# Attention states in 64-column tiles and cross products in 64x64 tiles, with two head pairs swapped and four reorderings, in a fused retention and SwiGLU-like block

## The chip, the core and the metric

The kernel runs on one core of a Trainium2 chip. The core has a matrix engine (TensorE, PE in the profile, with its weight loads shown as PEld), three elementwise engines (VectorE, DVE; ScalarE, ACT; GpSimd, POOL) and SyncE (SP), which here issues nearly all DMAs. The metric is the device time of one execution in microseconds. Before the change it is 308.35 us, the median of three runs (308.25 to 308.38).

## The reference

`q`, `k`, `v` have 8 batches, 8 heads, 576 positions and 64 columns. The reference is a retention layer followed by a two-matrix block:

```python
scores = q @ k.T / sqrt(64)
ret    = scores * gamma[h] ** (s - t)   for s >= t, else 0      # gamma[h] = 1 - 2 ** (-5 - h)
x      = ret @ v                        # laid out as (8 * 576) rows of 8 heads * 64 columns
h      = x @ w_in                       # 512 -> 2048
out    = (h * sigmoid(beta * h)) @ w_out  # 2048 -> 512
```

Since the decay is a power, `gamma ** (s - t)` splits into a factor of the query row and one of the value row. So the first 512 positions of a batch can be done in four chunks of 128 with a running state: the output of a chunk is its own masked product plus `q` times the sum of `k.T @ v` over the chunks before it.

## The kernel before

**Tiles.** A batch has four chunks (`CB = 4`); the last 64 positions of the eight batches are gathered in pairs into four "tail" blocks of 128 rows, entries `(None, c)` of the list `seq`. The two-matrix block works on 512 rows at a time: `up` (line L430) makes 16 tiles of the hidden layer, four matmuls of 512 columns each, and ScalarE evacuates each with a Silu (L432); `down` (L463) makes 4 row tiles of the output, 16 matmuls of 512 columns each. Heads are kept in four pairs `p`, each pair filling 128 partitions; `j` is the head within a pair.

**One batch of attention.** For chunk `i`: `pre` casts `k` to `kn` and scales `v` to `vn` (POOL, L279 and L261), `pre_q` scales `q` (L253), and a DMA transpose (`x_q`, `x_k`, L287) or PE (`t_q`, `t_k`) turns them. `a_sc` (L329) makes scores with 64 rows of contraction per head, DVE masks them into `R` (L334). `a_st` (L413) adds `kn.T @ vn` to the state in PSUM: one matmul of 128x128 per head pair, of which only the two 64x64 blocks on the diagonal are wanted. ACT copies these two blocks (L418, one copy for each `j`) into `sbds` or, after the last chunk, `ends`; those tiles are zero off the diagonal. `a_O` (L385) makes the chunk's own product, 64 output columns per head. `a_cross` (L371) adds `q` times the state, one 128x128 block-diagonal matmul per pair. `a_x` (L401) copies the sum to `xT`, which `up` reads. The tails use `ends` of two batches (L368).

**Order.** The order on every engine is written out by hand. `fill` is a list of `up` and `down` steps; `merged` walks it and, before step number n, runs all attention steps whose due number is n or less. `u1` is the number at which the `up` steps of batch 1 begin, `d0` that of the `down` steps of batch 0, `base[n]` that of the n-th block. While block n is computed, the attention of batch n+1 is woven in: `first` (state and scores of two chunks) and `outputs` (the products of all four chunks). Batches 0 and 1 have their own hand-written order.

**Loads.** SP issues DMAs in program order. At the start it loads `q`, `k`, `v` of batch 0, then `w_in` in seven pieces (L176), then `w_out` in four (L194), each into a ring of four buffers, then batch 1 and so on. A piece of `w_in` is cast by DVE and POOL (L190) as four slices `ko` of 128 rows; `ko` is also the head pair that the slice multiplies.

Of the kernel before, what the change touches and what calls it, by code (L numbers as in the profile page):

```python
# [11 lines left out]
F32 = mybir.dt.float32  # L12
BF16 = mybir.dt.bfloat16
# [6 lines left out]
def kernel(  # L20
# [10 lines left out]
    nc = tc.nc  # L31
    B, H, S, D = q.shape
# [3 lines left out]
    P = 128  # L36
    HP = H // 2
    KO = d_model // P
# [12 lines left out]
    seq = []  # L51
# [19 lines left out]
    QB = 2  # L71
    q_tiles, kv_tiles = {}, {}

    def load_q(b):

        if b >= B:
            return
        t = stage.tile([P, H, CB, D], F32, name="qn", tag="qn", bufs=2)
        for u in range(2):
# [3 lines left out]
        q_tiles[b] = t  # L83

    def load_kv(n, js=(0, 1)):

# [61 lines left out]
    causal2 = consts.tile([P, P], BF16, name="causal2")  # L148

    NS = 3  # L150
    sbds = [consts.tile([P, HP, P], BF16, name=f"sbd{i}") for i in range(NS)]
    ends = [consts.tile([P, HP, P], BF16, name=f"end{i}") for i in range(4)]
    for s in sbds + ends:
        nc.vector.memset(s[:], 0.0)


    w_in_sb = wpool.tile([P, KO, d_ff], BF16, name="w_in_sb")
# [125 lines left out]
    def heads(t, p):  # L283
        return t[:, 2 * p:2 * p + 2, :].rearrange("p h d -> p (h d)")
# [63 lines left out]
    def O_of(i, p):  # L348
        Os = live[i]["O"]
        return Os[p // 2][:, p % 2] if split(i) else Os[0][:, p]  # L350

    def opens(i, p):
        return p == 0 or split(i) and p == 2

    def a_cross(i, first):

        b, c = seq[i]
        if first:
            new_O(i)
        if c == 0 and b is not None:  # L360
            return
        for p in range(HP):
            rhs, view = q_cols(i, slice(0, P), p)
            O = O_of(i, p)
            if b is None:
                for x in range(2):
                    r = slice(x * TL, (x + 1) * TL)
                    nc.tensor.matmul(O[:, r], ends[(2 * c + x) % 4][:, p, :], rhs[:, r],  # L368
                                     start=False, stop=True, skip_group_check=True)
            else:  # L370
                nc.tensor.matmul(view(O), sbds[(c - 1) % NS][:, p, :], rhs,  # L371
                                 start=first and opens(i, p), stop=not first, skip_group_check=True)

    def a_O(i):

        b, c = seq[i]
        L = live[i]

        early = i < E
        if not early:  # L380
            new_O(i)
        R, vn = L["R"], L["vn"]
        crossed = b is None or c > 0
        for j, p in [(n // HP, n % HP) if early else (n % 2, n // 2) for n in range(H)]:
            nc.tensor.matmul(O_of(i, p)[j * D:(j + 1) * D], vn[:, 2 * p + j, :], R[:, j, p, :],  # L385
                             start=opens(i, p) and not (early and crossed), stop=early or not crossed,
                             skip_group_check=True)

# [14 lines left out]
    def a_st(i):  # L403

        b, c = seq[i]
        if b is None:
            return
        L = live[i]
        if c == 0:
            state_ps[b] = psum.tile([P, HP, P], F32, name="st", tag="st", bufs=1)  # L410
        st = state_ps[b]
        for p in range(HP):
            nc.tensor.matmul(st[:, p, :], heads(L["kn"], p), heads(L["vn"], p),  # L413
                             start=(c == 0 and p == 0), stop=True, skip_group_check=True)
        s = ends[b % 4] if c == CB - 1 else sbds[c % NS]
        for j in range(2):
            r = slice(j * D, (j + 1) * D)
            nc.scalar.copy(s[r, :, j * D:(j + 1) * D], st[r, :, j * D:(j + 1) * D])  # L418


    gts = {}
# [34 lines left out]
    def down(m, ms, f0, fn=4, n0=0, nn=d_model):  # L456

        gT = gts[m]
        if f0 == 0:
            pos_[ms] = psum.tile([P, d_model], F32, name="po", tag="mm", bufs=3)  # L460
        po = pos_[ms]
        for fo in range(f0, f0 + fn):
            nc.tensor.matmul(po[:, :nn], gT[:, fo, ms, :], w_out_sb[:, fo, n0:n0 + nn],  # L463
                             start=(fo == 0), stop=(fo == FO - 1))
        if f0 + fn < FO:
            return
        if ms == 0:
            ots[m] = stage.tile([P, MB // P, d_model], F32, name="ot", tag="wt", bufs=4)
        ot = ots[m][:, ms, n0:n0 + nn]
        (nc.scalar.copy if m == 0 else nc.vector.tensor_copy)(ot, po[:, :nn])  # L470
        if m < B:
            rows = out[m * S:m * S + MB].rearrange("(s i) n -> s i n", i=CB)
            if m < 2:
                held.append((rows[:, ms, n0:n0 + nn], ot))
            else:
                nc.sync.dma_start(rows[:, ms, n0:n0 + nn], ot)
        else:
            for x in range(2):
                r0 = (2 * ms + x) * S + MB
                nc.sync.dma_start(out[r0:r0 + TL, n0:n0 + nn], ot[x * TL:(x + 1) * TL])  # L480
# [12 lines left out]
    def F(f, *a):  # L493
        return lambda: f(*a)
# [76 lines left out]
    def second(i):  # L571
        for f in (a_O, lambda j: a_cross(j, False), a_x):
# [16 lines left out]
                (d0 + 15, F(a_st, 4)), (d0 + 15.9, F(second, 4))],  # L589
               [(d0 + 10, F(pre, 6, (0,))), (d0 + 10, F(pre, 7, (0,))), (d0 + 12, F(pre, 6, (1,))), (d0 + 12, F(pre, 7, (1,))),  # L590
                (d0 + 15.95, F(t_k, 6)), (u1 + 1, F(t_k, 7)), (u1 + 2, F(a_sc, 6)), (u1 + 3, F(a_sc, 7)),
                (u1 + 4, F(a_st, 6)), (u1 + 8, F(second, 6))]]


    def first(i):
        a_st(i)
        a_sc(i)
        a_sc(i + 1)

    def outputs(i):  # L600
        for f in (a_O, lambda j: a_cross(j, False), a_x):
            for j in range(i, i + CB):
                f(j)
        a_st(i + CB - 1)

    def pair_prep(i, at):
        b, c = seq[i]
        if b is None:
            return [(at - 31, F(load_tail, c)), (at - 21.5, F(pre, i)), (at - 21, F(load_tail, c + 1)),
                    (at - 13, F(pre, i + 1)), (at - 12, F(x_tail, i)), (at - 9.5, F(x_tail, i + 1))]  # L610
        n, st = full.index(i), []
        if b == XB:
# [3 lines left out]
            return [(u1 + 8 + x / 2, F(pre, i + x)) for x in range(2)] + [(u1 + 18.5, F(x_k, b, 1))]  # L616
        if c == 0:
            st += [(at - 30, F(load_q, b))] + [(at - 20 + x, F(pre_q, b, x)) for x in range(4)]
            st += [(at - 14 + 1.5 * x, F(x_q, b, x)) for x in range(2)]
        early = b == XB + 1 and c > 0  # L620
        return st + [(at - (25.4 if early else 28), F(load_kv, n)), (at - (25.3 if early else 26), F(load_kv, n + 1)), (at - 16, F(pre, i)),
                     (at - 15, F(pre, i + 1)), (at - 10.5, F(x_k, b, c // 2))]

    todo = list(range(2 * CB, len(seq), 2))
    for n in range(1, B - 1):

        take = [i for i in todo if seq[i][0] == n + 1 or n == B - 2 or seq[i] == (None, 0) and n == CB - 1]
        todo = todo[len(take):]
        lo, hi = (base[n] + 17, base[n + 1] - 7.5) if n == 1 else (base[n] + 3, base[n + 1] - 8)
        at = [lo + x * (hi - lo) / (len(take) - 1) for x in range(len(take))]  # L630
        if len(take) == 2 and n > 1:
            at[1] -= 6
        for i, t in zip(take, at):
            st = pair_prep(i, t) + [(t, F(first, i))]
            if seq[i][0] is None:
                st.append((t + 5, F(second, i)))
            elif seq[i][1] == 0:
                st.append((t + 2, F(a_st, i + 1)))
            else:
                st.append((t + 5, F(outputs, i - 2)))  # L640
            streams.append(st)
    assert not todo
# [31 lines left out]
```

## Time and profile before

| | |
|---|---|
| median of 3 runs | 308.35 us |
| profiled execution | 308.57 us |
| its span | 306.7 us |
| PE busy | 296.6 us, 97% |
| ACT, DVE, POOL busy | 141.8, 105.1, 99.1 us |
| granted PE clock | 1.0 |
| matmuls of `up` and `down` (L430, L463) | 126.6 and 127.0 us busy |
| states L413, cross products L371, own products L385, scores L329 | 12.4, 7.3, 10.8, 10.8 us busy |

The span runs from the first to the last instruction of the profiled execution; 1.87 us lie around it. "Busy" of PE counts the stretches in which at least one matmul is under way, and the end of a matmul is modelled, so that two matmuls that follow each other at once overlap in it. The chain of waits, which follows the work that ended last back from the end, gives each group from its last start to the next and adds up without overlap; the prediction takes its durations from there. A few per cent of the matmul records are missing from a trace, so a group can count fewer matmuls than the code has.

### The profile page before, as it was taken

The page shows a single profiled execution, that of the slowest core. Times are in us where ns is not written, and L with a number is a line of the kernel's source. Part 1 is how long each engine was busy: PE and PEld are TensorE (multiplying, and loading weights), DVE is VectorE, ACT ScalarE, POOL GpSimd, SP SyncE. Part 2 cuts the span into 40 slices and gives each one's busy share as a digit, 9 for nine tenths or more (in the row PEclk, how much of TensorE's full clock was granted, in tenths as well). Part 3 has the DMA queues.
Part 4 walks back from the last instruction along what each step waited for, and adds up shares of the span by engine and source line. Part 5 has one row for each costly group of instructions (what it writes and reads, how often), then busy time and mean ns, then how long its engine had stood idle before and what let it go on. Part 6 is the DMA issues. An engine that isn't in the chain of part 4 may idle for free.

```text
span 306.7 us, 5306 instructions
## 1 busy us (share of the span) xinstructions
PE 296.6 (97%) x2113; PEld 155.6 (51%) x2145; DVE 105.1 (34%) x190; ACT 141.8 (46%) x251; POOL 99.1 (32%) x136
## 2 busy tenths in 40 slices
PE   7799999999999999999999999999999999999995
PEld 5554456855554454554554545454545444444444
DVE  7554556304550433234430623052414420020012
ACT  5577546882168313650286208710773047207700
POOL 4665117654643264354326031912330000000000
PEclk9999999999999999999999999999999999999999
DMA  8999999999999999999995499939990110131012
GB/s 210 218 348 381 380 238 257 217 191 230 185 274 171 249 266 227 214 257 186 193 246 88 103 211 267 174 83 196 196 148 4 76 61 0 25 77 36 0 68 71
DMA packets 128697, 53.84 MB, mean 176 GB/s; under 512 B 109968, under 2 KB 121632, under 8 KB 128672
## 3 DMA queue, kind: packets, MB, share of 16 engines
q1 hardware_dynamic: 128640, 53.49, 79.2%
q8 instruction: 17, 0.28, 0.4%
q14 instruction: 8, 0.07, 0.1%
q10 hardware_dynamic: 32, 0.01, 0.0%
HBM read 36.71 MB, written 9.44 MB: 150 GB/s over the span
## 4 chain that ended last, share of the span: by engine, by line
PE 90%; DMA 4%; SPq 2%; issue 1%; ACT 1%; DVE 1%; POOL 1%
PE ph L430 40%; PE po L463 38%; PE sc L329 3%; PE O L385 3%; DMA kT<-kn 2%; PE O L371 2%; PE st L413 2%; DMA kvn<-in_k_dram 2%; SPq L94 2%; PE ph L445 1%; PE T L309 1%; ACT gT L432 0%; ACT kT L310 0%; PE O L368 0%; POOL vn L261 0%
## 5 line engine op out<-in xcount | busy, mean ns | idle before, releaser
L432 ACT ACTIVATE gT<-ph,beta_sb 128x512 bf16<-128x512 f32 (+1 forms) x152 | 99.1, 659 | 80.7 <-PE ph L430 80.2
L463 PE MATMUL po<-w_out_sb,gT 128*128 128x512 bf16 (+2 forms) x591 | 127.0, 368 | 1.5 <-ACT gT L432 0.3
L430 PE MATMUL ph<-xT,w_in_sb 128*128 128x512 bf16 (+1 forms) x594 | 126.6, 365 | 0.9 <-ACT gT L432 0.2
L430 PEld LDWEIGHTS <-w_in_sb 128*128 128x128 bf16 x608 | 58.1, 98 | 62.2 <-DVE w_in_sb L190 0.9
L463 PEld LDWEIGHTS <-gT 128*128 128x128 bf16 x608 | 57.0, 98 | 63.1 <-issue 0.6
L334 DVE TENSOR_TENSOR R<-sc,causal 128x512 bf16<-128x512 f32 x72 | 44.9, 683 | 76.3 <-PE sc L329 76.2
L470 DVE COPY ot<-po 128x512 f32<-128x512 f32 (+2 forms) x34 | 22.4, 659 | 84.8 <-PE po L463 84.8
L261 POOL TENSOR_TENSOR vn<-kvn,gv 128x512 bf16<-128x512 f32 x32 | 33.3, 1044 | 19.4 <-DMA kvn<-in_v_dram 10.1
L279 POOL CAST kn<-kvn 128x512 bf16<-128x512 f32 x32 | 19.6, 614 | 44.7 <-DMA kvn<-in_k_dram 39.8
L253 POOL TENSOR_TENSOR qs<-qn,gq 128x512 bf16<-128x512 f32 x24 | 24.3, 1044 | 28.8 <-DMA qn<-in_q_dram 28.8
L418 ACT CAST sbd<-st 64x256 bf16<-64x256 f32 x48 | 17.4, 364 | 20.6 <-PE st L413 20.0
L401 DVE CAST xT<-O 128x512 bf16<-128x512 f32 x24 | 15.7, 687 | 19.7 <-PE O L385 10.5
L401 ACT CAST xT<-O 128x512 bf16<-128x512 f32 x10 | 5.9, 587 | 31.1 <-PE O L371 31.0
L413 PE MATMUL st<-vn,kn 128*128 128x128 bf16 x128 | 12.4, 219 | 0.2 <-POOL vn L261 0.2
L413 PEld LDWEIGHTS <-kn 128*128 128x128 bf16 x128 | 9.2, 98 | 4.7
L329 PE MATMUL sc<-qT,kT 64*128 64x128 bf16 x256 | 10.8, 218 | 0.9 <-ACT kT L310 0.6
L385 PEld LDWEIGHTS <-vn 128*64 128x64 bf16 x288 | 8.5, 109 | 4.5 <-issue 3.6
L385 PE MATMUL O<-R,vn 128*64 128x128 bf16 x288 | 10.8, 221 | 0.0
L268 POOL TENSOR_TENSOR kn<-tln,gq 128x512 bf16<-128x512 f32 x4 | 4.2, 1043 | 20.1 <-DMA tln<-in_q_dram 20.1
L329 PEld LDWEIGHTS <-kT 64*128 64x128 bf16 x288 | 8.2, 94 | 4.7 <-issue 1.7
L190 POOL CAST w_in_sb<-wt 128x256 bf16<-128x256 f32 (+1 forms) x13 | 6.4, 510 | 4.9 <-DMA wt<-in_moe_w_in_dram 4.9
L214 PE MATMUL ph<-warm 128*128 128x128 f32 (+1 forms) x24 | 6.7, 412 | 1.2 <-DVE warm L119 1.2
(61 smaller groups left out, 91.1 us busy)
## 6 DMA issues: line engine op xcount, KB each, us to landing
qn<-in_q_dram SPq DMA_DIRECT2D x16, 512.0 KB, 5.6
kvn<-in_k_dram SPq DMA_DIRECT2D x32, 256.0 KB, 5.1
kvn<-in_v_dram SPq DMA_DIRECT2D x32, 256.0 KB, 5.2
out_dram<-ot SPq DMA_DIRECT2D x31, 256.0 KB, 3.2
wt<-in_moe_w_out_dram SPq DMA_DIRECT2D x4, 1024.0 KB, 10.0
wt<-in_moe_w_in_dram SPq DMA_DIRECT2D x6, 512.0 KB, 8.4
out_dram<-ot SPq DMA_DIRECT2D x9, 128.0 KB, 2.4
wt<-in_moe_w_in_dram SPq DMA_DIRECT2D x4, 256.0 KB, 5.9
```

The source lines that it names most:

```text
L253: e.tensor_tensor(batch[b]["qs"][:, cs, hs], q_tiles[b][:, hs, cs].rearrange("p h i d -> p i h d"), gq[:, cs, hs].unsqueeze(3).to_broadcas ...
L261: nc.gpsimd.tensor_tensor(live[i]["vn"][:], kv_tiles.pop(i)[:, 1], gains(gv, c), ALU.mult)
L279: nc.gpsimd.tensor_copy(kn[:, c % 2], t[:, 0])
L329: nc.tensor.matmul(view(sc[j][:, p, :]), L["kT"][r, p, :], rhs, start=True, stop=True, skip_group_check=True)
L334: nc.vector.tensor_tensor(R[:, j], sc[j][:], m_b, ALU.mult)
L385: nc.tensor.matmul(O_of(i, p)[j * D:(j + 1) * D], vn[:, 2 * p + j, :], R[:, j, p, :], start=opens(i, p) and not (early and crossed), stop= ...
L401: (nc.scalar.copy if on_act else nc.vector.tensor_copy)(x, view(Os[0]))
L413: nc.tensor.matmul(st[:, p, :], heads(L["kn"], p), heads(L["vn"], p), start=(c == 0 and p == 0), stop=True, skip_group_check=True)
L430: nc.tensor.matmul(ph, w_in_sb[:, ko, fo * P:(fo + 1) * P], xts[m][:, ko, :, w], start=(ko == 0), stop=(ko == KO - 1))
L432: nc.scalar.activation(gts[m][:, fo, :, w], ph, ACT.Silu, scale=beta_sb[:, fo:fo + 1])
L463: nc.tensor.matmul(po[:, :nn], gT[:, fo, ms, :], w_out_sb[:, fo, n0:n0 + nn], start=(fo == 0), stop=(fo == FO - 1))
L470: (nc.scalar.copy if m == 0 else nc.vector.tensor_copy)(ot, po[:, :nn])
```

## The change

From batch 2 on (`b >= QB`), the state of a pair is made by two matmuls of 64 output columns with 64 moving columns each, one for each head, so that both heads' blocks lie in the same 64 columns of PSUM and one ACT copy of 128 partitions takes them to `sbq`. The cross product of a pair becomes two matmuls of 64 rows by 64 columns. `crosses` issues them in fours: heads `j = 0` and `j = 1` of pair `p` write the lower and the upper half of the output partitions, those of pair `p + 2` the other way round. For this the heads of pairs 2 and 3 are swapped in the output rows, in all batches, and the rows of `w_in` that multiply them are swapped when they are loaded: each piece is loaded by one DMA for `ko` 0 and 1 and two DMAs of 64 partitions for `ko` 2 and 3. Two chunks share a PSUM bank (`O4`), and `x4` copies two banks for each. `ends` and the remaining `sbds` have ten slots of 64 columns, in which two slots make a block.

The four reorderings: `down_rows` does row tiles 0 and 1 first and 2 last; `second(6)` of batch 1 is due one step earlier, and the state copy of chunk 6 goes from ACT to DVE; the state of chunk 1 joins the one before the scores of chunks 2 and 3 (`first`), that of chunk 2 goes to the head of `outputs`, and that of chunk 3 ahead of the cross products; the DMA transpose `x_k(XB, 1)` is issued between the two halves of the load of `q` of batch 3, and the two pairs of chunks of batch 2 are due two steps earlier at their end (`- 9.5`).

```diff
-        for w in (slice(0, 2), slice(2, KO)) if g in (0, 1, NP - 1) else (slice(0, KO),):
-            nc.sync.dma_start(t[:, w], w_in_r[:, w, f0:f0 + fn])
+        for r, x, w in ((0, 0, slice(0, 2)), (0, D, slice(2, KO)), (D, 0, slice(2, KO))):
+            n = D if w.start else P
+            nc.sync.dma_start(t[r:r + n, w], w_in_r[x:x + n, w, f0:f0 + fn])
...
+    def block(s, p):
+        f = 2 * p
+        return s[:, f:f + 2].rearrange("k h d -> k (h d)")
...
-        for j, p in [(n // HP, n % HP) if early else (n % 2, n // 2) for n in range(H)]:
-            nc.tensor.matmul(O_of(i, p)[j * D:(j + 1) * D], vn[:, 2 * p + j, :], R[:, j, p, :],
+        for hh, p in [(n % 2, n // 2) for n in range(H)]:
+            j = hh ^ p // 2
+            nc.tensor.matmul(O_of(i, p)[hh * D:(hh + 1) * D], vn[:, 2 * p + j, :], R[:, j, p, :],
...
+            if tiled:
+                for j in range(2):
+                    nc.tensor.matmul(st[j * D:(j + 1) * D, p, :D], L["kn"][:, 2 * p + j, :], L["vn"][:, 2 * p + j, :],
+                                     start=(c == 0 and p == 0), stop=True, skip_group_check=True)
...
+        if tiled and c < CB - 1:
+            nc.scalar.copy(sbq[c % NS][:], st[:, :, :D])
+            return
...
+    def crosses(i):
+        for c in range(1, CB):
+            for p, x in [(p, x) for p in range(2) for x in range(4)]:
+                r, hh, p = slice(x % 2 * D, x % 2 * D + D), x % 2 ^ x // 2, p + x // 2 * 2
+                rhs, _ = q_cols(i + c, r, p)
+                nc.tensor.matmul(out4(i + c, p, hh), sbq[c - 1][r, p, :], rhs, start=False, stop=True, skip_group_check=True)
+    def x4(i):
+        b = seq[i][0]
+        for c, u in ((0, 0), (0, 1), (1, 0), (1, 1)):
+            (nc.scalar.copy if (c, u) == (0, 1) else nc.vector.tensor_copy)(
+                xt(b)[:, 2 * u:2 * u + 2, :, 2 * c * PC:2 * (c + 1) * PC], live[i]["O4"][c, u][:])
...
-        for x in range(4 * n, 4 * n + 4):
-            down(0, x % 3, x // 3, 1)
+        for fo, ms in [(2 * n + x // 2, x % 2) for x in range(4)] if n < 2 else [(fo, 2) for fo in range(4)]:
+            down(0, ms, fo, 1)
...
-                (u1 + 4, F(a_st, 6)), (u1 + 8, F(second, 6))]]
+                (u1 + 4, F(a_st, 6)), (u1 + 7, F(second, 6))]]
...
     def first(i):
-        a_st(i)
+        a_st(i - (seq[i][1] == 2 and seq[i][0] is not None))
...
     def outputs(i):
-        for f in (a_O, lambda j: a_cross(j, False), a_x):
-            for j in range(i, i + CB):
-                f(j)
-        a_st(i + CB - 1)
+        a_st(i + 2)
+        for j in range(i, i + CB):
+            a_O4(j)
+        a_st(i + 3)
+        crosses(i)
+        x4(i)
...
-            return [...] + [(u1 + 18.5, F(x_k, b, 1))]
+            return [...]
...
-            st += [(at - 30, F(load_q, b))] + ...
+            st += [(at - 30, F(load_q, b, (0,)))] + ([(at - 30, F(x_k, XB, 1))] if b == XB + 1 else [])
+            st += [(at - 30, F(load_q, b, (1,)))] + ...
...
-        lo, hi = (base[n] + 17, base[n + 1] - 7.5) if n == 1 else ...
+        lo, hi = (base[n] + 17, base[n + 1] - 9.5) if n == 1 else ...
...
-            elif seq[i][1] == 0:
-                st.append((t + 2, F(a_st, i + 1)))
```

`a_O4` is `a_O` for the shared banks; it opens a bank with the first matmul of its even chunk.

More of the change, by code (lines that the diff above doesn't have):

```diff
@@ L72, with load_q @@
     q_tiles, kv_tiles = {}, {}
-    def load_q(b):
+    def load_q(b, us=(0, 1)):
         if b >= B:
             return
-        t = stage.tile([P, H, CB, D], F32, name="qn", tag="qn", bufs=2)
-        for u in range(2):
+        if 0 in us:
+            q_tiles[b] = stage.tile([P, H, CB, D], F32, name="qn", tag="qn", bufs=2)
+        t = q_tiles[b]
+        for u in us:
             w = slice(u * HP, (u + 1) * HP)
@@ L82, in load_q @@
                               q[b, w, :MB, :].rearrange("h (p i) d -> p h (i d)", i=CB))
-        q_tiles[b] = t
     def load_kv(n, js=(0, 1)):
@@ L150 @@
     NS = 3
-    sbds = [consts.tile([P, HP, P], BF16, name=f"sbd{i}") for i in range(NS)]
-    ends = [consts.tile([P, HP, P], BF16, name=f"end{i}") for i in range(4)]
+    sbds = [consts.tile([P, 10, D], BF16, name=f"sbd{i}") for i in range(1)]
+    ends = [consts.tile([P, 10, D], BF16, name=f"end{i}") for i in range(4)]
+    sbq = [consts.tile([P, HP, D], BF16, name=f"sbq{i}") for i in range(NS)]
     for s in sbds + ends:
         nc.vector.memset(s[:], 0.0)
+    sbds += ends[2:]
     w_in_sb = wpool.tile([P, KO, d_ff], BF16, name="w_in_sb")
@@ L367, in a_cross @@
                     r = slice(x * TL, (x + 1) * TL)
-                    nc.tensor.matmul(O[:, r], ends[(2 * c + x) % 4][:, p, :], rhs[:, r],
+                    nc.tensor.matmul(O[:, r], block(ends[(2 * c + x) % 4], p), rhs[:, r],
                                      start=False, stop=True, skip_group_check=True)
             else:
-                nc.tensor.matmul(view(O), sbds[(c - 1) % NS][:, p, :], rhs,
+                nc.tensor.matmul(view(O), block(sbds[(c - 1) % NS], p), rhs,
                                  start=first and opens(i, p), stop=not first, skip_group_check=True)
@@ L410, in a_st @@
             state_ps[b] = psum.tile([P, HP, P], F32, name="st", tag="st", bufs=1)
-        st = state_ps[b]
+        st, tiled = state_ps[b], b >= QB
         for p in range(HP):
-            nc.tensor.matmul(st[:, p, :], heads(L["kn"], p), heads(L["vn"], p),
-                             start=(c == 0 and p == 0), stop=True, skip_group_check=True)
+            if tiled:
+                for j in range(2):
+                    nc.tensor.matmul(st[j * D:(j + 1) * D, p, :D], L["kn"][:, 2 * p + j, :], L["vn"][:, 2 * p + j, :],
+                                     start=(c == 0 and p == 0), stop=True, skip_group_check=True)
+            else:
+                nc.tensor.matmul(st[:, p, :], heads(L["kn"], p), heads(L["vn"], p),
+                                 start=(c == 0 and p == 0), stop=True, skip_group_check=True)
@@ L415, in a_st @@
+        if tiled and c < CB - 1:
+            nc.scalar.copy(sbq[c % NS][:], st[:, :, :D])
+            return
         s = ends[b % 4] if c == CB - 1 else sbds[c % NS]
         for j in range(2):
-            r = slice(j * D, (j + 1) * D)
-            nc.scalar.copy(s[r, :, j * D:(j + 1) * D], st[r, :, j * D:(j + 1) * D])
+            r, w = slice(j * D, (j + 1) * D), slice(0, D) if tiled else slice(j * D, (j + 1) * D)
+            (nc.vector.tensor_copy if i == CB + 2 else nc.scalar.copy)(
+                s[r, slice(1, 7) if j else slice(0, 10)].rearrange("k (u y) d -> k u y d", u=2)[:, :, 0:3:2], st[r, :, w].rearrange("k (u y) d -> k u y d", u=2))
@@ new lines, in crosses, with out4 @@
+    def crosses(i):
[4 more added lines that the diff above has]
+                nc.tensor.matmul(out4(i + c, p, hh), sbq[c - 1][r, p, :], rhs, start=False, stop=True, skip_group_check=True)
+    def out4(i, p, hh):
+        c = seq[i][1]
+        return live[i - c]["O4"][c // 2, p // 2][hh * D:(hh + 1) * D, p % 2, :, c % 2 * PC:(c % 2 + 1) * PC]
@@ new lines, in a_O4 @@
+    def a_O4(i):
+        c, L = seq[i][1], live[i]
+        if c == 0:
+            L["O4"] = {}
+        if c % 2 == 0:
+            for u in range(2):
+                live[i - c]["O4"][c // 2, u] = psum.tile([P, 2, CB, 2 * PC], F32, name="O", tag="sc" if c else "O", bufs=2)
+        for n in range(H):
+            hh, p = n % 2, n // 2
+            j = hh ^ p // 2
+            nc.tensor.matmul(out4(i, p, hh), L["vn"][:, 2 * p + j, :], L["R"][:, j, p, :].rearrange("k (i s) -> k i s", i=CB),
+                             start=c % 2 == 0 and p % 2 == 0, stop=False, skip_group_check=True)
@@ L615, in pair_prep @@
                        [(d0 + 14, F(pre, i + x, (1,))) for x in range(2)]
-            return [(u1 + 8 + x / 2, F(pre, i + x)) for x in range(2)] + [(u1 + 18.5, F(x_k, b, 1))]
+            return [(u1 + 8 + x / 2, F(pre, i + x)) for x in range(2)]
         if c == 0:
-            st += [(at - 30, F(load_q, b))] + [(at - 20 + x, F(pre_q, b, x)) for x in range(4)]
+            st += [(at - 30, F(load_q, b, (0,)))] + ([(at - 30, F(x_k, XB, 1))] if b == XB + 1 else [])
+            st += [(at - 30, F(load_q, b, (1,)))] + [(at - 20 + x, F(pre_q, b, x)) for x in range(4)]
             st += [(at - 14 + 1.5 * x, F(x_q, b, x)) for x in range(2)]
@@ L628 @@
         todo = todo[len(take):]
-        lo, hi = (base[n] + 17, base[n + 1] - 7.5) if n == 1 else (base[n] + 3, base[n + 1] - 8)
+        lo, hi = (base[n] + 17, base[n + 1] - 9.5) if n == 1 else (base[n] + 3, base[n + 1] - 8)
         at = [lo + x * (hi - lo) / (len(take) - 1) for x in range(len(take))]
@@ L636 @@
                 st.append((t + 5, F(second, i)))
-            elif seq[i][1] == 0:
-                st.append((t + 2, F(a_st, i + 1)))
-            else:
+            elif seq[i][1] > 0:
                 st.append((t + 5, F(outputs, i - 2)))
```

## The prediction

> **What bounds the kernel now.** I read the page first: PE is busy 97% of the span at full clock, so what counts is PE time, and stalls of PE. The groups say what the attention part takes:
>
> ```profile
> PE 296.6 (97%) x2113; PEld 155.6 (51%) x2145; DVE 105.1 (34%) x190; ACT 141.8 (46%) x251; POOL 99.1 (32%) x136
> L413 PE MATMUL st<-vn,kn 128*128 128x128 bf16 x128 | 12.4, 219 | 0.2 <-POOL vn L261 0.2
> ```
>
> Busy time overlaps, so I take durations from the chain of waits, where each group runs to the next one's start. The window from 69 us holds one batch's attention:
>
> ```profile
> 69.30 0.22 PE st L413 x4
> 69.52 0.60 PE sc L329 x16
> 70.12 0.01 issue
> 70.14 1.01 POOL vn L261
> 71.15 6.47 DMA kT<-kn
> 77.62 0.05 issue
> 77.67 0.62 PE sc L329 x16
> ...
> 82.71 1.01 PE O L385 x32
> 83.72 0.78 PE O L371 x12
> 84.50 0.22 PE st L413 x4
> ...
> 86.45 2.59 PE ph L430 x12
> 89.04 0.22 PE st L413 x4
> 89.26 0.55 PE sc L329 x16
> 89.82 1.83 PE ph L430 x8
> ```
>
> A matmul of 512 columns takes 2.59/12 = 0.216 us, a full 128-column one 0.22/4 = 55.5 ns. Two half-size tiles run side by side: 32 own products take 1.01 and 16 take 0.57 (56.44 in the same view), so 27.5 ns each and 0.13 for the change of shape. Likewise sc: 0.55 - 16 x 0.0275 = 0.11; cross: 0.78 - 12 x 0.0555 = 0.11; back to 512 columns: 1.83 - 8 x 0.216 = 0.10. So **every change of tile shape costs PE about 0.11 us**. After 60 us PE has only one real stall, at 77.6, where scores wait for the transposed keys (kT). Before that, two stalls stand at 55 and 58 us; PE's timeline has them:
>
> ```profile
> 54.20 1.47 PE L430 MATMUL ph<-xT,w_in_sb 128*128 128x256 bf16 x12
> 55.84 0.60 PE L430 MATMUL ph<-xT,w_in_sb 128*128 128x256 bf16 x4 [0.17 <-ACT gT L432]
> ```
>
> Twelve half-width matmuls at 0.109 us end their starts at 55.51; the next comes at 55.84: 0.33 lost, since ACT makes two state copies between two Silus (chain: `sbd` at 54.55 and 54.92). At 58.72 the chain shows `up` waiting for an xT copy; eight matmuls from 57.62 would be through at 58.49: 0.23 lost.
>
> From 2 to 63 us the loads never pause, and PE follows them closely; four stretches give their rates (last figure of a row, GB/s):
>
> ```profile
> 6.00:14.00 8.00, 5.87 (x76) 4.09 (x76) 4.65 (x8) 4.10 (x8) 5.30 (x9) 1.00 1.38 219
> 18.00:23.00 5.00, 4.67 (x22) 1.85 (x24) 2.36 (x8) 3.59 (x7) 2.55 (x7) 1.00 1.10 350
> 220.90:221.80 0.90, 0.90 (x6) 0.43 (x5) 0.00 (x0) 0.85 (x3) 0.00 (x0) 1.00 1.23 271
> 267.25:268.55 1.30, 1.30 (x8) 0.59 (x7) 0.00 (x0) 0.00 (x0) 0.00 (x0) 1.00 0.76 175
> ```
>
> They are k/v loads (256 B packets, 128 partitions), w_in (1 KB, 128 partitions), two tail loads (256 B, 64 partitions each), two tail stores (2 KB, 64 partitions).
>
> **The change part by part.** *Steady part, batches 2 to 7.* Before, PE spends per batch, apart from sc and O: four states 0.88, cross 12 x 0.0555 = 0.67, six changes of shape 0.66: 2.21 us. After there are nine changes (into the state's shape, to sc, back, twice; into state/O, to cross, back): 0.99. A state is eight matmuls of half width with 64 moving columns. Unseen; the tail's cross products have 64 moving columns at full width, 16 in 0.57 (126.21), so 28 ns, and two tiles at once would make 14. A cross matmul is a quarter of the array: 55.5/4 = 13.9 ns if four overlap, 27.5 if only two do. I take the low ends, since sc (two row tiles) and O (two column tiles) both overlap fully: 32 x 0.014 + 24 x 0.0139 = 0.78, total 1.77. Gain 0.44 a batch, **-2.64 us**. At the high ends 56 x 0.0275 = 1.54, total 2.53: +0.32 a batch, +1.92.
>
> A rule speaks against this. The Trainium skill, "TensorE: Matmul & The Clock Gate", section "Wait — 56ns, not 53.3ns?", says that starts of matmuls never come closer than about 25 ns, however few the columns. The shortest mean here is 27.5 ns, so no row contradicts it. By it, as an estimate, 56 x 25 ns + 0.99 = 2.39, or +1.1 us over six batches.
>
> *ACT and DVE.* 18 state copies become one instead of two of 0.364: ACT saves 6.6 us, off the path. The state of chunk 3 now has to wait in `outputs` for the copy of chunk 2's (about 0.37 and 0.1 of signalling); 32 O matmuls (1.01) lie between. Cover gone: 0.1 or less a batch. What queues behind it is the cross products alone. x4's three DVE copies (0.69 each) start together after the crosses and end some 2.1 us later; 36 `down` matmuls (7.7 us) cover them, in batch 2 now 16 (3.45) where 8 were. Cost 0.
>
> *Batch 1.* With chunk 6's copy on DVE no copy stands between those Silus: -0.33. `second(6)` one step (0.44) earlier leaves three `up` steps (1.31) before xT is needed: -0.23. DVE's two copies (about 0.4 each) follow its last mask at 55.2 and end near 56.0; the cross product that needs them comes near 56.5. Bounds: -0.56 to 0; I take -0.56.
>
> *x_k on SP.* It moves ahead of half a load of q and of three k/v loads, but waits on SP for POOL's kn cast (68.96 + 0.61), with that half load and all behind it queued. From 69.7 it lands after 3.3 to 6.5 us (landings of transposes here), I take 4.4, so 74.1 (the page's median, 5.0, gives 74.7). The scores, two `down` steps and 0.56 earlier, want it near 75.0. The stall of 0.20 (77.67 against 77.15 + 0.22 + 0.10) goes: **-0.20**; at 6.5 it is +1.2. The q of batch 3 arrives some 2 us later; its keys' transpose landed at 84.8, sc uses them at 89.3 (88.1 after): still about 1 us spare.
>
> *down_rows.* Before, the third matmul waits for a PSUM buffer from 32.95 to 33.68. After, the third needs the second cast row of w_out, on DVE from 32.38 to 33.64. Same time: 0 (to -0.5 if that cast ran in 0.48 like its neighbours).
>
> *w_in loads.* Ten DMAs become 21 on SP, about 0.52 each: 10.9 us, while the data take 13, so issue does not bind. Unseen: 64 partitions at 1 KB. Low, the same rate, 0. High, the stores' 175 GB/s: 128 KB in 0.75 instead of 0.375, 12 times, and 256 KB in 1.5 instead of 0.68, twice: 6.1 us later. Nearest are the tail loads, same direction and queue: 271 GB/s, no slower than 128 partitions with such packets (219). So I take no slowdown, and 0.2 us for more and smaller DMAs. Casts and transposes of batch 1 have about 0.5 us to spare behind the loads; PE pays what exceeds it. Casts of ko 0 and 1 can start half a piece sooner, but the w_out wait just named swallows that. **+0.2**.
>
> The Trainium skill, "SBUF — State Buffer", section "Can I just issue two DMAs to hit both halves?", says that loads to two halves of the partitions serialize on half the ports, 218 GB/s. The stores agree, the 271 does not. By it, as an estimate, w_in comes 3.7 us later and PE pays 3.2.
>
> *No cost:* the O order and DVE memsets of the start (five of 0.34 for seven of 0.27) hide behind waits for k and q loads; the copies into slots move the same 64x256 elements as before (0.364).
>
> Sum: -2.64 - 0.56 - 0.20 + 0.20 = -3.2. The profiled execution took 308.57 (span 306.7 and 1.87 around), 0.22 over the median; it would take 305.4, and the median goes to **305.2**.
>
> **The rivals.** *Small tiles do not overlap.* Place: states and crosses; price as above, +1.92 with the rest -0.56: 309.7, slower. It decides where 56 t + 0.99 exceeds 2.21 + 0.56/6, at a mean t of 23.5 ns. Against: O and sc overlap two by two. For: no group here holds four tiles or more than 48 matmuls in a row, and `outputs` will have 72 with their weight loads, so supply of instructions may bind too.
>
> *64-partition loads are slow.* 6.1 - 0.5 = 5.6 at the stores' rate, -3.4 of the rest: 310.6; halfway 307.8. For: the stores. Against: the tail loads.
>
> *The stalls move.* x_k lands late, or DVE's copies are late: -2.64 + 0.2, with 0 to +1.2: 305.9 to 307.1.
>
> **How the numbers follow.** Forecast 0.45 (own range 304.4 to 306.3); small tiles 0.25 (305 to 309.7, mostly above 307); slow loads 0.20 (306 to 310.6); stalls 0.10. Range 304.4 to 309.4: below it lies a gain of the casts and of `down_rows` together, above it the worst fifth of two rivals. 0.2%, 0.6 us, is what a measurement can tell. Faster: 0.45 + 0.06 + 0.06 + 0.08 = 0.65; same 0.12; slower 0.23.
>
> **What would show it.** States of 8 in about 0.11 and crosses of 24 in about 0.45 us with their change of shape; 0.22 and 0.78 would say rival one. L430 ending near 32.7 us, not 35 or later, says that the loads hold. No ACT copy between Silus near 55 us, no wait for kT near 75. Wrong it would be if a change of shape into 64x64 cost far more than 0.11.

## The result, and the profile after

The changed kernel takes **312.43 us** (median of four runs, 311.35 to 313.2) against 308.3 for the kernel before beside it: a ratio of 1.013, 95% interval 1.0104 to 1.0155. It is slower; 305.2 was forecast. Two of the four runs took 311.35 and 311.66, at a mean granted clock of 1.0, and two 313.2, at 0.99; the profiled one is of the second kind (313.19, span 311.5).

The page of the changed kernel, second part, shows where: PEclk drops once, in the fifth and sixth slices, and in the third and fourth the loads run at 237 and 248 GB/s, where the kernel before had 348 and 381.

```profile
span 311.5 us, 5673 instructions
...
PEclk9999689999999999999999999999999999999999
...
GB/s 211 225 237 248 328 369 193 272 200 204 231 176 267 236 246 228 233 234 166 222 233 186 17 219 253 218 53 226 187 179 9 67 69 0 2 92 42 0 55 82
```

In the fifth part the weight loads of `up` (PEld) now wait 5.9 us in all for a cast of w_in by DVE, and its matmuls 3.2. The last line is the kernel before, with 0.9 us for the weight loads.

```profile
L482 PE MATMUL ph<-xT,w_in_sb 128*128 128x512 bf16 (+1 forms) x608 | 130.6, 371 | 4.6 <-DVE w_in_sb L194 3.2
...
L482 PEld LDWEIGHTS <-w_in_sb 128*128 128x128 bf16 x608 | 58.7, 99 | 70.6 <-DVE w_in_sb L194 5.9
...
L430 PEld LDWEIGHTS <-w_in_sb 128*128 128x128 bf16 x608 | 58.1, 98 | 62.2 <-DVE w_in_sb L190 0.9
```

The timeline of PE from 29 to 42 us has the two long waits, with their releasers in brackets. Behind the second, 14 matmuls take 5.79 us, 0.41 each instead of 0.216.

```profile
33.29 0.89 PE L482 MATMUL ph<-xT,w_in_sb 128*128 128x512 bf16 x2 [2.16 <-DVE w_in_sb L194]
35.53 5.79 PE L482 MATMUL ph<-xT,w_in_sb 128*128 128x512 bf16 x14 [1.34 <-DVE w_in_sb L192]
```

The stretches say why (length; busy us of PE, PEld, DVE, ACT and POOL with instructions; granted clock; DMA share; GB/s): PE was busy 1.13 us of three, and after that its clock was 0.67 and 0.60. These two are means: in the last two rows, of 1 us each, the clock falls from 1.00 to 0.50 at 34 us, and the same query shows 0.50 up to 40 us, 0.59 for the next microsecond and 1.00 from 41 us on.

```profile
30.00:33.00 3.00, 1.13 (x6) 0.29 (x3) 0.19 (x1) 1.48 (x3) 0.16 (x1) 1.00 1.05 223
33.00:36.00 3.00, 1.28 (x4) 0.47 (x5) 0.94 (x3) 0.00 (x0) 1.50 (x3) 0.67 1.04 332
36.00:42.00 6.00, 6.00 (x18) 2.25 (x17) 3.44 (x6) 2.70 (x5) 1.17 (x2) 0.60 1.05 387
...
33.00:34.00 1.00, 0.62 (x2) 0.19 (x2) 0.24 (x1) 0.00 (x0) 0.71 (x1) 1.00 1.04 258
34.00:35.00 1.00, 0.18 (x1) 0.00 (x0) 0.00 (x0) 0.00 (x0) 0.00 (x0) 0.50 1.03 350
```

The chain of waits gives the whole account in time. It runs through the last w_in load, which lands at 35.09 us (before: 29.17), to `down` at 41.32 (before: 33.68), the first transposes of batch 1 at 51.68 (before: 43.77) and then into the new attention groups:

```profile
26.59 8.49 DMA wt<-in_moe_w_in_dram
...
41.32 10.36 PE po L515 x48
51.68 0.45 PE T L307 x8
...
76.83 0.24 PE st L424 x8
77.07 0.55 PE sc L333 x16
...
89.28 0.12 PE st L424 x8
89.40 0.46 PE O L444 x24
...
308.71 0.29 DVE ot L522
```

The same places in the chain of the kernel before (that of 69.30 stands in the prediction):

```profile
33.68 8.36 PE po L463 x38
...
43.77 0.45 PE T L303 x8
...
303.57 0.29 DVE ot L470
```

So the difference splits without a rest. Up to the transposes: +7.91. From there to the first state of batch 2: 25.15 against 25.53, -0.38. From there to the last copy: 231.88 against 234.27, -2.39. Sum +5.14, which is 308.71 less 303.57; the spans differ by 4.8, since what follows the last copy is 0.3 shorter. So the attention part did gain 2.77 of the 3.40 that was forecast for it, and the start, with the loads of w_in, lost almost three times that gain.

### The profile page after: what moved, and what is told of

Same layout as the page of the kernel before. It is cut to its first block, busy times and chain, and to the rows that moved or that the text cites. A ratio compares the mean times of both kernels' runs of the same rounds, so it can differ in the third digit from the quotient of the medians.

```text
span 311.5 us, 5673 instructions
## 1 busy us (share of the span) xinstructions
PE 300.4 (96%) x2313; PEld 152.7 (49%) x2313; DVE 104.3 (33%) x190; ACT 135.6 (44%) x231; POOL 99.3 (32%) x136
## 4 chain that ended last, share of the span: by engine, by line
PE 88%; SPq 8%; DMA 3%; issue 0%; DVE 0%; DVEq 0%
PE po L515 40%; PE ph L482 38%; SPq L180 4%; SPq L95 3%; PE sc L333 3%; DMA wt<-in_moe_w_in_dram 3%; PE O L462 2%; PE st L424 2%; PE O L444 1%; PE O L394 1%; PE O L376 0%; PE st L427 0%; SPq L83 0%; PE T L313 0%; PE T L307 0%
## 5 line engine op out<-in xcount | busy, mean ns | idle before, releaser
L484 ACT ACTIVATE gT<-ph,beta_sb 128x512 bf16<-128x512 f32 (+1 forms) x152 | 99.5, 659 | 94.3 <-PE ph L482 94.1
L482 PE MATMUL ph<-xT,w_in_sb 128*128 128x512 bf16 (+1 forms) x608 | 130.6, 371 | 4.6 <-DVE w_in_sb L194 3.2
L515 PE MATMUL po<-w_out_sb,gT 128*128 128x512 bf16 (+2 forms) x608 | 129.0, 368 | 0.0
L430 ACT CAST sbq<-st 128x256 bf16<-128x256 f32 x18 | 6.6, 369 | 43.1 <-PE st L424 43.1
L469 DVE CAST xT<-O 128x512 bf16<-128x512 f32 x18 | 11.3, 685 | 15.6 <-PE O L444 15.6
L435 ACT CAST end<-st 64x256 bf16<-64x256 f32 x22 | 8.1, 367 | 5.3 <-PE st L424 3.7
L424 PEld LDWEIGHTS <-kn 128*64 128x64 bf16 x192 | 5.1, 111 | 7.6 <-issue 5.5
L210 DVE TENSOR_SCALAR w_out_sb<-wt,rbeta_sb 128x512 bf16<-128x512 f32 x12 | 6.0, 556 | 6.1 <-DMA wt<-in_moe_w_out_dram 6.1
L194 DVE CAST w_in_sb<-wt 128x256 bf16<-128x256 f32 (+1 forms) x13 | 3.9, 305 | 10.7 <-DMA wt<-in_moe_w_in_dram 10.7
L424 PE MATMUL st<-vn,kn 128*64 128x64 bf16 x192 | 7.4, 200 | 0.0
```

The costliest lines, as they stand in the source:

```text
L424: nc.tensor.matmul(st[j * D:(j + 1) * D, p, :D], L["kn"][:, 2 * p + j, :], L["vn"][:, 2 * p + j, :], start=(c == 0 and p == 0), stop=True, ...
L469: (nc.scalar.copy if (c, u) == (0, 1) else nc.vector.tensor_copy)(xt(b)[:, 2 * u:2 * u + 2, :, 2 * c * PC:2 * (c + 1) * PC], live[i]["O4"] ...
L482: nc.tensor.matmul(ph, w_in_sb[:, ko, fo * P:(fo + 1) * P], xts[m][:, ko, :, w], start=(ko == 0), stop=(ko == KO - 1))
L484: nc.scalar.activation(gts[m][:, fo, :, w], ph, ACT.Silu, scale=beta_sb[:, fo:fo + 1])
```

## The experiments

The theory after reading the two traces, L: the two DMAs of 64 partitions per piece delay w_in, and nothing else in the change costs time. Its rivals: S, other reorderings of the start cost it; N, it is the number of DMAs, not their shape; X, it is where the rows lie in memory.

**The kernel after with the old loads.**

```diff
-        for r, x, w in ((0, 0, slice(0, 2)), (0, D, slice(2, KO)), (D, 0, slice(2, KO))):
-            n = D if w.start else P
-            nc.sync.dma_start(t[r:r + n, w], w_in_r[x:x + n, w, f0:f0 + fn])
+        for w in (slice(0, 2), slice(2, KO)) if g in (0, 1, NP - 1) else (slice(0, KO),):
+            nc.sync.dma_start(t[:, w], w_in_r[:, w, f0:f0 + fn])
```

> The kernel after with w_in loaded by the ten DMAs of before, 128 partitions each. The rows of w_in for pairs 2 and 3 are then not swapped, so heads 4 to 7 meet the weights of their neighbour; the amount of work is that of the kernel after. Theory L (the loads of 64 partitions delay w_in and with it the first batch, all else gains): the first transposes of batch 1 come near 43.8 us instead of 51.68, the 2.8 us gained behind them stay: 308.3 - 2.8 = 305.5 us, 305.0 to 306.3. Rival S (the reorderings of the start, that is the order of O, of down_rows or the memsets, cost it, and the loads only wait with them): 311 to 313, as the kernel after.

Measured: 305.81 us (305.3 to 307.22), ratio 0.9931 (0.9905 to 0.9956). All of the loss is gone with the loads; S falls. The stretch from 23 to 27 us, in the kernel before, in the kernel after and in this run:

```profile
23.00:27.00 4.00, 4.00 (x20) 1.88 (x20) 1.92 (x6) 2.91 (x6) 2.34 (x6) 1.00 1.06 374
23.00:27.00 4.00, 3.47 (x16) 1.30 (x15) 1.18 (x4) 2.51 (x4) 2.09 (x4) 1.00 1.12 251
23.00:27.00 4.00, 4.00 (x21) 1.84 (x20) 1.86 (x6) 3.10 (x6) 2.28 (x5) 1.00 1.07 372
```

The profiled run was the slowest of the four, 307.22, and its chain shows two waits that are not in the kernel after. The last load of w_out took 10.65 us and landed at 40.87, as `down` reached it (transposes at 44.54 instead of 43.77), and scores waited for transposed keys:

```profile
30.22 10.65 DMA wt<-in_moe_w_out_dram
...
44.54 0.45 PE T L306 x8
...
135.89 6.18 DMA kT<-kn
142.12 0.62 PE sc L332 x16
```

**The kernel before with loads of 64 partitions.** The same three DMAs a piece, 21 in all, rows in their order:

```diff
-        for w in (slice(0, 2), slice(2, KO)) if g in (0, 1, NP - 1) else (slice(0, KO),):
-            nc.sync.dma_start(t[:, w], w_in_r[:, w, f0:f0 + fn])
+        for r, x, w in ((0, 0, slice(0, 2)), (0, 0, slice(2, KO)), (D, D, slice(2, KO))):
+            n = D if w.start else P
+            nc.sync.dma_start(t[r:r + n, w], w_in_r[x:x + n, w, f0:f0 + fn])
```

> The kernel before with one edit: ko 2 and 3 of each piece of w_in come in two DMAs of 64 partitions, rows not swapped, 30 DMAs less the halves that the shorter list of pieces saves. Theory L: last w_in near 35 instead of 29.17 us, start of down near 41 instead of 33.7, 308.3 + 7.5 = 315.8 us, 314 to 317. Rival S: no more than 0.3 us over the kernel before, 308.3 to 308.6, since the start is otherwise that of before. Rival X (the swap of the rows, that is where the data lie in memory, slows the loads, not the 64 partitions): 308.3 to 309 too.

Measured: 314.8 us (314.12 to 316.22), ratio 1.0221 (1.0193 to 1.0248). The edit alone costs 6.55 us; S and X fall. Rates in two stretches, then the chain: the last piece lands at 35.96 and `down` is at 41.93 where the kernel before is at 33.68.

```profile
18.00:23.00 5.00, 4.13 (x20) 1.47 (x20) 1.67 (x6) 2.83 (x6) 1.62 (x5) 1.00 1.02 214
23.00:27.00 4.00, 3.17 (x13) 0.97 (x11) 1.18 (x4) 2.19 (x4) 2.03 (x4) 1.00 1.13 206
```

```profile
27.89 8.07 DMA wt<-in_moe_w_in_dram
...
36.40 4.77 PE ph L431 x14
...
41.93 10.09 PE po L464 x46
```

**The kernel before with as many DMAs, all of 128 partitions.**

```diff
-        for w in (slice(0, 2), slice(2, KO)) if g in (0, 1, NP - 1) else (slice(0, KO),):
+        for w in (slice(0, 2), slice(2, 3), slice(3, KO)):
```

> The kernel before with one edit: as many DMAs of w_in as in the kernel after (three a piece: ko 0 and 1, ko 2, ko 3) of the same bytes, but all over 128 partitions. Theory L (it is the 64 partitions): last w_in near 29 us, 308.3 us, 308.0 to 309.0. Rival N (it is the number of DMAs, their issue on SP at 0.6 us each and their fixed costs): last w_in near 34 us, 313 to 316, as the run with 64 partitions.

Measured: 310.45 us (309.24 to 311.43), ratio 1.0064 (1.0033 to 1.0094). Neither theory had this: the number alone costs 2.2 of the 6.55 us, and the step to 64 partitions the other 4.35. The last w_in lands at 30.82 us, 1.65 later than in the kernel before. The rate lies between:

```profile
18.00:23.00 5.00, 4.72 (x28) 2.21 (x26) 3.21 (x10) 3.62 (x7) 3.46 (x10) 1.00 0.92 281
23.00:27.00 4.00, 4.00 (x20) 1.85 (x19) 1.25 (x5) 3.12 (x6) 1.85 (x4) 1.00 0.97 280
```

The share of the DMA engines helps to tell the two apart. Divided by the rate it is the engines' time for a byte. Set against the kernel before (1.10 at 350, 1.06 at 374), this time is 1.04 and 1.22 times as long here, and the share is lower, which points to pauses between the DMAs. With 64 partitions it is 1.5 and 1.9 times as long, at a share of 1.02 and 1.13: the engines are occupied and slow. That the pauses make the 2.2 us was not tested.

**Half of the 64-partition DMAs on another queue.** If one half of the partitions is slow, two halves at once from two queues could be as fast as 128.

```diff
-        for r, x, w in ((0, 0, slice(0, 2)), (0, D, slice(2, KO)), (D, 0, slice(2, KO))):
+        for r, x, w in ((0, 0, slice(0, 2)), (0, D, slice(2, KO))):
...
+        nc.scalar.dma_start(wts[g][D:, 2:KO], w_in_r[:D, 2:KO, f0:f0 + fn])
```

> The kernel after with the third DMA of each piece of w_in (ko 2 and 3, upper 64 partitions) on ACT's queue instead of SP's, so that the two halves can be under way together. The seven issues delay ACT at the start, so the run's time says little; the rates between 18 and 30 us are what is looked at. Theory H (one transfer of 64 partitions is slow since it uses one half of the partitions only; both halves at once are as fast as 128 partitions): 330 to 380 GB/s there instead of 240 to 253, last w_in near 30 us. Rival Q (the rate is lost whatever runs beside it): 230 to 270 GB/s.

Measured: 318.5 us, in one run. ACT's seven issues, placed behind its copy of the first keys, kept it from 8.61 to 23.78 us, so the start is some 14 us late and the time says nothing. The rates do, since SP's w_in DMAs (12.82 to 27.87 us) and ACT's were issued side by side: no faster than on one queue (240 to 253 in the kernel after).

```profile
8.61 15.17 ACTq L185 DMA_DIRECT2D wt<-in_moe_w_in_dram  x7
```

```profile
18.00:23.00 5.00, 0.00 (x0) 0.00 (x0) 0.00 (x0) 0.00 (x0) 2.18 (x4) 0.50 1.13 222
23.00:27.00 4.00, 1.70 (x20) 1.51 (x20) 1.06 (x2) 1.90 (x5) 2.12 (x7) 0.50 1.12 241
27.00:30.00 3.00, 2.63 (x34) 1.77 (x33) 1.51 (x3) 2.14 (x5) 0.80 (x2) 0.69 1.11 212
```

The loads issued in these stretches are those of w_in alone. H falls, and the rates lie at the lower end of Q's range and below it. The Trainium skill, "SBUF — State Buffer", section "Can I just issue two DMAs to hit both halves?", says just this: only one transfer over all 128 partitions reaches all ports, and a second issuing engine does not help. The run agrees.

This run also bears on a rival that no theory above names: the time that SP takes to issue a DMA. With 64 partitions it is 0.60 us, in the run of 128 partitions 0.43 (medians; kernel after, then that run):

```profile
L180 SPq DMA_DIRECT2D wt<-in_moe_w_in_dram x21: 594/602/1392, 12.2 to 26.6; - x21
L176 SPq DMA_DIRECT2D wt<-in_moe_w_in_dram x21: 328/433/1396, 12.1 to 24.3; - x21
```

In the kernel after, the chain of waits runs along these issues without a gap, from 12.20 us to the last one at 26.59. Three of them for a piece of 512 KB allow some 270 GB/s (an estimate: 3 x 0.64 us, with the 0.04 between them), little more than the 240 to 253 that the stream moved. With seven of the issues on ACT the rate was no higher, so slow transfers are enough to hold it down. How the 4.35 us divide between transfers and issue is not shown.

**Idle matmuls in the waits.** Is the slow clock the pause's doing?

```diff
         for ko in range(KO):
+            if m == 0 and fo == 12 and ko in (0, 2):
+                for _ in range(14 if ko == 0 else 9):
+                    nc.tensor.matmul(cold[:, :256], warm[:, :P], warm[:, :256], start=True, stop=True, skip_group_check=True)
             nc.tensor.matmul(ph, w_in_sb[:, ko, fo * P:(fo + 1) * P], xts[m][:, ko, :, w],
```

> The kernel after with 23 idle matmuls (their result is not used) in the two longest waits of PE for w_in, 2.3 us at 30.75 and 1.5 us at 33.76. The data come as late as in the kernel after. Theory C (the pause itself lowers PE's clock: 14 matmuls then take 5.79 us instead of 3.02): every run near 311.0, the page shows full clock from 33 to 42 us, down starts near 38.6 instead of 41.3. Rival (the clock falls for another reason, or the idle matmuls delay the real ones): 312 to 313.5, with two groups of runs 1.7 us apart, as the kernel after.

Measured: 317.19 us (316.83 to 318.15). The filler was too long: a float32 matmul of 256 columns stands in the trace as two instructions of 0.22 us, so the 23 took 10.1 us and PE was 4 us late. Still, the 14 matmuls behind them took 3.02 us:

```profile
31.98 6.04 PE cold L486 x28
...
38.29 4.05 PE cold L486 x18
42.34 3.02 PE ph L487 x14
```

With five and three in place of 14 and 9:

> The kernel after with 8 idle matmuls instead of the 23 of the earlier run, whose 46 passes took 10.1 us (0.22 us a pass, two passes each) and so delayed PE by 4 us: now five in the wait at 30.75 us (2.15 us) and three in that at 33.76 (1.3 us). Theory C (the pause lowers PE's clock): full clock from 33 to 42 us, the 14 matmuls after the last piece of w_in in 3.0 us instead of 5.79, down from about 38.6 us, all runs near 311.0. Rival (nothing is gained, since w_in binds): 311.3 to 313.2 in two groups, as the kernel after.

Measured: 312.69 us (312.01 to 313.38). Full clock throughout, `down` at 39.07 and the transposes of batch 1 at 49.65, 2.03 us sooner than in the kernel after:

```profile
36.00:42.00 6.00, 5.82 (x28) 2.48 (x27) 3.44 (x6) 3.47 (x5) 1.13 (x2) 1.00 1.04 385
```

The mean granted clock is 0.999 or 1.0 in all eight runs with filler; in two of four runs each of the kernel after and of the kernel before with loads of 64 partitions it is 0.988 to 0.995. So PE's pauses do lower the clock, though not in every run, and C is right on that. But the time is that of the kernel after. In the profiled run (312.01) `down` now waits until 39.07 us for a cast of w_out, and 0.8 us went into a wait of scores for transposed keys at 146 us that the kernel after does not have; where the rest went in the slower runs stays open.

**The swap moved from w_in to POOL.** The old loads need the rows of w_in in their order. So from batch 2 on, POOL writes the heads of pairs 2 and 3 of q and k swapped.

```diff
+    def slots(op, dst, src):
+        for d, s in ((slice(0, 4), slice(0, 4)), (slice(5, 8, 2), slice(4, 8, 2)), (slice(4, 8, 2), slice(5, 8, 2))):
+            op(dst[:, d], src[:, s], s)
...
-        nc.gpsimd.tensor_copy(kn[:, c % 2], t[:, 0])
+        if swapped(i):
+            slots(lambda o, x, s: nc.gpsimd.tensor_copy(o, x), kn[:, c % 2], t[:, 0])
```

> The kernel after without any swap of w_in: its loads are the ten of before, and from the third batch on POOL writes the scaled q and the cast k with the heads of pairs 2 and 3 swapped (three instructions instead of one, for 24 chunks of q, 24 of k and three tail pairs), so that states and cross products still fall on four 64x64 tiles and O comes out in the natural order. Batches 0 and 1 keep the order of before. Theory L: 305.5 us, 305.0 to 306.5, faster than both kernels. Rival P (POOL, at 99 us busy before, now some 30 us longer, delays the keys' transposes and PE waits for scores): 307 to 310.

Measured: 307.13 us (306.34 to 307.69), ratio 0.9957 (0.9941 to 0.9974): faster than before, but outside L's range and at the low edge of P's. PE's waits for keys are 2.2 us here (0.9 with the old loads), and POOL stands in the chain ahead of a transpose. How much of this is POOL's doing is not shown.

```profile
PE sc L351 <- DMA kT<-kn: 2.2, 2, 1.3
```

```profile
116.31 0.82 POOL kn L299 x3
...
135.59 6.69 DMA kT<-kn
```

**Other slots, one instruction each.** A permutation that one access pattern can write: head 4j + p in slot 2p + j. Both heads of a pair of slots then go to one column half, and pairs alternate.

```diff
+    def slots(t):
+        return t.rearrange("s (p j) d -> s j p d", j=2)
+    def by_head(t):
+        return t.rearrange("s (j p) d -> s j p d", j=2)
...
+            nc.gpsimd.tensor_copy(slots(kn[:, c % 2]), by_head(t[:, 0]))
...
-        if tiled and c < CB - 1:
-            nc.scalar.copy(sbq[c % NS][:], st[:, :, :D])
+        if tiled:
+            nc.scalar.copy((sbq[c % NS] if c < CB - 1 else ends[b % 4])[:], st[:, :, :D])
```

> The tiles of the kernel after with the loads of before, and no more instructions on POOL than before: from the third batch on, the one instruction that scales a chunk of q or casts one of k also writes the heads in another order, head 4j + p in slot 2p + j. So both heads of a pair of slots go to the same column half, the two pairs to different halves, and states and cross products again fill four 64x64 tiles; a state needs one copy in every chunk, and the cross products of the last three tail pairs are 64x64 as well. w_in is in its natural order. Theory L (only the loads of w_in cost the kernel after its gain, and POOL's extra instructions took 1.3 us in the run with slots swapped): 305.8 us as with the old loads, or a little less, 305.0 to 306.2. Rival P (the swap on POOL has no part in that 1.3 us, which is a wait for transposed keys that moves with every change): 306.5 to 307.5.

Measured: 306.38 us (305.16 to 306.87), ratio 0.9932 (0.9907 to 0.9958). The medians lie 0.75 us under the run before and the intervals overlap; in the profiled run the only wait for keys left is about 0.2 us.

> As the run before in this call, with two DMA transposes issued earlier on SP: the keys of chunks 2 and 3 of batch 4 ahead of the second pair of k/v loads of batch 5, and the second tail's right behind the first's. Theory K (with the loads of w_in mended, what is left over the predicted 305.2 is the wait for these keys, 1.09 us at 141 us and, with the slots swapped, 1.09 at 119): 0.5 to 1.2 us less than the run before, 304.3 to 305.3. Rival (the transposes land no earlier, since the transfers, not SP's order, bind): the same as the run before within 0.3 us.

Measured: 306.3 us (305.25 to 306.59). This run tested nothing: moving the due times from 119.5 to 115.3 and from 99.5 to 97.1 left both transposes behind the same loads, and the order of work on SP, ACT, DVE and POOL is that of the run before. It, its repeat beside the next run and the run before are therefore 14 runs of one program: 305.16 to 306.87, median 306.0.

**The spread.** Two candidates: the last load of w_out, and the keys.

```diff
-        nc.sync.dma_start(t[:], w_out_r[:, g * KO:(g + 1) * KO, :])
+        for x in ((0, 2), (2, KO)) if g == WG - 1 else ((0, KO),):
+            nc.sync.dma_start(t[:, x[0]:x[1]], w_out_r[:, g * KO + x[0]:g * KO + x[1], :])
```

> The kernel with reordered slots and the two transposes moved, with the last load of w_out in two DMAs of two rows of blocks each. Theory W (the spread of these kernels, 305.2 to 306.9, is the last load of w_out: it landed at 40.50 and 40.87 us in two profiled runs of 306.1 and 307.2 and PE waited 0.8 us, and at 39.6 to 39.7 in others, with no wait): its first half lands a microsecond sooner, no wait near 41 us, all runs near 305.3, 305.0 to 305.8. Rival (the spread has another cause): median 306.2 and the spread as before.

> The kernel of two DMA transposes moved, run again beside the one with the last load of w_out in two DMAs, as its control on the same chip. Theory W: 306.3 us as measured, 0.5 to 1 over the other. Rival (the spread has another cause): the same as the other within 0.3 us.

Measured: 305.99 (305.32 to 308.1) with the load split, 305.68 (305.3 to 306.69) without. The split is no faster and its spread no smaller, so W falls. Both profiled runs had no wait at 41 us and one at 140, for the keys (the control; us in total, times, longest):

```profile
PE sc L350 <- DMA kT<-kn: 1.1, 2, 0.8
```

So, last, two transposes really sooner on SP: those keys with their casts ahead of batch 5's q and k/v, and the first tail's ahead of batch 4's q.

```diff
+        a, z, y = (19.5, 19.4, 19.1) if (b, c) == (XB + 2, 2) else (16, 15, 10.5)
...
-                     (at - 15, F(pre, i + 1)), (at - 10.5, F(x_k, b, c // 2))]
+                     (at - z, F(pre, i + 1)), (at - y, F(x_k, b, c // 2))]
...
-(at - 12, F(x_tail, i)), (at - 9.5, F(x_tail, i + 1))]
+(at - (19.6 if c == 0 else 12), F(x_tail, i)), (at - (11.9 if c == 0 else 9.5), F(x_tail, i + 1))]
```

> The kernel with reordered slots, with two DMA transposes truly earlier in SP's order: the keys of chunks 2 and 3 of batch 4 ahead of the load of q and the first two pairs of k/v of batch 5 (in the run with two transposes moved they stayed behind them), their casts on POOL just before, and the first tail's keys ahead of the load of q of batch 4. Theory K (the rest and the spread of these kernels is PE's wait for transposed keys, 0.1 to 1.3 us at 140 us and 0 to 1.1 at 119): those two waits go, all runs near 305.2, 304.9 to 305.6. Rival (what is late moves on: q of batches 4 and 5, 1.3 us later, makes PE wait at 119 or 150 us): 305.7 to 306.5, as the kernels beside it.

Measured: **305.58 us** (305.18 to 306.39), ratio 0.9904 (0.9884 to 0.9924). It beats both kernels. The waits for keys are gone, and the transposes of batch 1 start at 43.77, where they do in the kernel before:

```profile
43.77 0.45 PE T L324 x8
...
119.36 0.55 PE sc L350 x16
...
140.32 0.24 PE st L449 x8
140.56 0.55 PE sc L350 x16
...
300.83 0.29 DVE ot L547
```

Whether that is worth more than the run-to-run spread is not shown: 305.58 against 306.0, with overlapping ranges.

## Why the prediction was wrong

**The step that failed is "w_in loads": +0.2 was taken, +7.91 measured.** The price was chosen between two ends, 0 and 6.1 us later, by the row that seemed nearest, the tail loads at 271 GB/s. The high end was near the true one, w_in came 5.92 us later, but partly by luck, as that end knew nothing of what the count of DMAs does (1.65 us by itself). Two things were wrong with the row. It is 0.90 us long, with the first two of six tail loads; the stretch right behind it, in which the rest of them and then transposes were under way, moved 172 GB/s (kernel before):

```profile
221.80:226.20 4.40, 4.40 (x22) 2.02 (x21) 0.00 (x0) 3.59 (x6) 1.66 (x2) 1.00 1.18 172
```

And it was nearest in direction, queue and partitions, but its packets are of 256 B, and such loads reach only 219 GB/s with 128 partitions too; so something else than the partitions seems to hold them (argued from these two rows; no run tested it), and they could not show what halving those costs a load that runs at 350 to 374. The stores, with packets of 2 KB at 175 GB/s, were the row to go by. The rule of the skill that the prediction weighed and set aside was right in kind (its 218 GB/s stands in the same page under "Door 1: The DMA port swizzle"): the estimate by it was 3.7 us for the delay. The number of DMAs, for which 0.2 was allowed, added 2.2 to the time by itself. And "issue does not bind" rested on 0.52 us for each of 21 issues, 10.9 in all; with 64 partitions they took 0.60, and the 21 of them 15.0 us.

**A second price was not in the prediction at all.** PE's waits for w_in lowered its clock: 14 matmuls in 5.79 us instead of 3.02, +2.77 in the profiled run. 5.92 and 2.77 make the 7.91 if 0.78 us were covered (0.5 was taken); the 0.78 is a remainder, not a measurement. Of the 2.77 not all counts: with filler the transposes come 2.03 us sooner, and the two runs that kept the clock are 1.7 us faster. Those two are still 3 us slower than the kernel before, so the late loads alone are enough to make the change a loss. The Trainium skill, "TensorE: Matmul & The Clock Gate", section "What's actually happening", tells of a gate that halves the clock after an idle window of about 3.4 us. The trace agrees with the half. It does not show an idle window: the clock fell at 34.0 us, after a wait of 2.16 us and before that of 1.34, and PE had been busy 1.16 us of the 3.4 before. So PE need not be idle throughout.

**Steady part and x_k: right, a little too high.** -2.84 forecast, -2.39 measured. A state's eight matmuls take 0.12 and 24 cross products 0.46 with their change of shape, as the signs named. Four 64x64 tiles do overlap: (0.46 - 0.11)/24 is 14.6 ns each, and the skill's floor of 25 ns between starts, weighed there at +1.1 us, does not hold for tiles. The wait for keys at 77 us is gone. The 0.45 missing was not located.

**Batch 1: the sign right, a third of it replaced.** -0.56 forecast, -0.38 measured. The Silu stall of 0.33 is gone. Of the xT wait of 0.23 a stall of 0.18 is left at 66.1 us, with another cause: ACT's two copies of the last state of batch 1 now stand ahead of a Silu that PE needs a buffer from. The timeline of the kernel after:

```profile
64.97 0.74 ACT L435 CAST end<-st 64x256 bf16<-64x256 f32 x2 [0.87 <-PE st L427]
65.73 1.20 ACT L484 ACTIVATE gT<-ph,beta_sb 128x256 bf16<-128x256 f32 x3
```

**down_rows, O order, memsets: right at 0.** In the last run, which has them with the old loads, the transposes of batch 1 start at 43.77 us as before (at 44.17 and 44.54 in two profiled runs where PE waited for the last load of w_out).

**The rivals.** "64-partition loads are slow" was the true one, and too cheap: 310.6 at its far end, since it knew neither the clock nor the price of the count. "Small tiles do not overlap" is refuted. "The stalls move" came true only once the loads were mended: the wait for keys near 140 us is 0.1 to 1.3 us in six of the seven profiled runs with mended loads.

With the loads of before, the other terms as measured give 308.57 - 0.38 - 2.39 = 305.8, and as forecast 305.2; the last run's profiled execution took 305.5, with the cross products of three tails also in 64x64 tiles and two transposes moved.

## What to carry to other kernels

A load cut along the partitions is not a smaller load. Here half of the bytes came in DMAs of 64 partitions, and the stream fell from 350 and 374 to 214 and 206 GB/s; if the other half kept its rate, that is 0.4 of the rate for the part that was cut, and 0.6 if the stream with as many uncut DMAs (281 and 280) is the measure (estimates). So put the permutation where an engine rewrites the data anyway, in the access pattern of a cast. When two rows of a trace bound a price, ask what limits each of them, and whether the row is long enough to be a rate: 0.90 us was not. A wait of PE in a busy stretch costs its length and can then cost the clock, so look at the granted clock behind every new wait.

## What the runs showed that was not expected

- Of 6.55 us that three DMAs a piece cost, 2.2 came with the count alone (281 GB/s, engines 0.92 busy), 4.35 with 64 partitions (206 to 214 GB/s, engines 1.02 to 1.13 busy, SP's issue 0.60 us instead of 0.43). Two queues did not help (212 to 241).
- In the profiled run a wait of 2.16 us, with a second of 1.34 behind it, left PE at half its clock from 34.0 to 40.8 us; two of four runs kept the clock. Filling the waits kept it at 1.00, and the median time did not fall with it.
- Tiles of 64x64 run four at once at 14.6 ns a matmul of 128 columns; each change of shape, into them too, is 0.09 to 0.13 us.
- With PE faster, loads become the next bound in places: the keys of batch 4 landed 0.1 to 1.3 us late in seven profiled runs whose PE came there sooner than in the kernel after, and not in the kernel after.
